# The first group of a fused mLSTM cell and feed-forward block: other landings, smaller turns and another order of loads

## The chip, the cores and the metric

The kernel runs on one core of a Trainium2 chip. The core has a matrix engine (TensorE, PE in the profile, with its weight loads as PEld), a vector engine (VectorE, DVE), an activation engine (ScalarE, ACT), a general engine (GpSimd, POOL) and a sync engine that mostly issues transfers (SyncE, SP). ScalarE issues transfers too; both queues are served by the core's 16 DMA engines. The metric is the device time of one execution in microseconds (us), lower is better.

## The reference

There are two blocks. The first is an mLSTM cell over B = 4 sequences, H = 8 heads, S = 768 steps, head size D = 40. The second is a feed-forward block (SwiGLU) on the 3072 tokens of width 320 that come out.

```python
for t in range(S):
    m_new = np.maximum(f_gate[:, :, t] + m, i_gate[:, :, t])
    f_stab = np.exp(f_gate[:, :, t] + m - m_new)
    i_stab = np.exp(i_gate[:, :, t] - m_new)
    m = m_new
    C = f_stab[..., None, None] * C + i_stab[..., None, None] * np.einsum('bhd,bhe->bhde', vt, kt)
    n = f_stab[..., None] * n + i_stab[..., None] * kt
    h_tilde = np.einsum('bhde,bhe->bhd', C, qt)
    nq = np.einsum('bhd,bhd->bh', n, qt)[:, :, None]
    denom = np.maximum(np.abs(nq), 1.0)
    o = 1.0 / (1.0 + np.exp(-o_gate[:, :, t]))
    y[:, :, t] = o * h_tilde / denom
...
x = y.transpose(0, 2, 1, 3).reshape(3072, 320)
g = x @ w_gate                                  # 320 x 1536
out = (g / (1 + np.exp(-g)) * (x @ w_val)) @ w_out   # 1536 x 320
```

The three weight matrices arrive as 64-bit floating point numbers, everything else in 32 bits.

## The kernel before

**Groups.** The kernel takes the 768 steps in six groups of 128 steps. A group is 128 steps of all four sequences, 512 tokens. Within a group the recurrence is written as matrix products: scores of keys against queries, weighted by a triangular matrix of exponentials (the intra part), plus the state that came in from the groups before. Each group then goes through the feed-forward block: twelve hidden steps m (128 of the 1536 hidden columns each), then the output projection.

**The order is written by hand.** A manual schedule is in force: every engine works through its instructions in the order in which the program names them, and each instruction waits on semaphores for what it needs. So a waiting instruction holds back all behind it on its engine, and the same is true for the transfers that an engine issues. Program order is therefore what sets the order of the work around the change.

**The first group** has no incoming state and is done by functions of its own (lines 520 to 665), which work on 16 (batch, head) pairs at a time, P = 0 and P = 1. Its parts:
- Transfers of k, q, v and o, 40 floats (160 bytes) per row, into tiles whose rows are padded: `k_sb` and `q_sb` have 64 columns per head, 40 used, `v_sb` has 41 with a one at the end.
- `first_mask`, `first_inputs`, `first_maxima` (531 to 541) put the exponents of the triangular weights in eight banks of PSUM, and `first_exp` (547) writes their exponentials to `W0`, which lies in the columns 0 to 7 of the tile `h_sb`.
- `first_turn` (561) transposes k and q on TensorE, two heads side by side, 128 rows at a time. Line 142 (ScalarE) or 144 (VectorE) copies the result out.
- `first_scores` (571) multiplies keys by queries, and line 575 multiplies the result into `W0`. `first_own` (582) multiplies `W0` by v, for one sequence u: 8 matmuls of 128 by 128.
- `first_x` (587 to 590) divides by the denominators, `sig` (515) takes the sigmoid of o, `first_gate` (596) multiplies by it and copies 64 columns behind the row as padding (597).
- `first_values` (552, 553) weights v by the last row, `first_state` (604) multiplies by k for the state that the next group gets, `first_kept` copies it out.
- `first_seam` (616) transposes x to `xT`, what the feed-forward block takes in.
- `burn` (521) are matmuls of no use to the result that keep TensorE at work; there are 7 at the start, and 3, 2 and 1 between the parts.

**The weights** are loaded in pieces (`piece_load`, 163 to 190): pieces 0 and 1 hold one hidden step each, 2 to 6 hold two each, 7 to 9 the output weights. The gate half of a piece goes to partitions 0 to 63, its val half, in two transfers, to partitions 64 to 127. SyncE issues the gate halves; ScalarE issues the val halves of pieces 0 to 4, SyncE those of 5 and 6. A piece lands as pairs of 32-bit words in one of two `raw` buffers, or, for pieces 2, 3 and 4, in parts of `h_sb` and `wo_sb` that are not yet in use. Then `convert` makes 32-bit floats of it: `scale` (ScalarE, 212 and 214), `join` (VectorE, 221 and 222), `rounded` (229, VectorE or GpSimd).

**The hidden steps** of the first group are the ten matmuls of line 706 for each m (20 rows of the profile, each over 512 tokens), the silu in 711, and the product in 712. `ahead[m]` names conversions and `slots[m]` all other work that goes between the steps: the loads for the second group, the late sums, maxima and decays of the state's scalars, and from slot 7 the weights of the second group. These are in `w_sb`: maxima go out to memory as `M_dram` (963), come back broadcast as two transfers (484), are subtracted (488), masked (493), taken to exponentials (512), multiplied by scores (360), and used by the `add` matmuls (379) between m = 10 and m = 11.

After the hidden steps comes `project_all` (723), and then the groups 1 to 5, which keep TensorE packed.

Of the kernel before, what the change touches and what calls it, by code (L numbers as in the profile page):

```python
# [24 lines left out]
def kernel(  # L25
# [135 lines left out]
    def piece_load(p, home=None):  # L161
        kind, m, n = PIECES[p]
        if kind == "gv":
            a, d = NKC, n * 128
            gate_w, val_w = (w[:, m * 128:(m + n) * 128].rearrange("(c p) f -> p c f", p=HP) for w in (moe_w_gate, moe_w_val))
            src = [(slice(0, HP), slice(0, NKC), gate_w), (slice(HP, 128), slice(0, NKC - 1), val_w[:, 1:]),
                   (slice(HP, 128), slice(NKC - 1, NKC), val_w[:, 0:1])]
            queues = (nc.sync,) + 2 * (nc.scalar if p < 5 else nc.sync,)
        else:
            a, d = n, DM  # L170
            src = [(slice(0, 128), slice(0, n), moe_w_out[m * 128:(m + n) * 128].rearrange("(a p) d -> p a d", p=128))]
            queues = (nc.sync,)
        if src[0][2].dtype == F32:
            for r, cs, w in src:
                if kind == "o":
                    nc.sync.dma_start(out=wo_sb[r, m:m + n, :], in_=w)
                else:
                    for x in range(n):
                        nc.sync.dma_start(out=wgv_sb[r, m + x, cs], in_=w[:, :, ts(x, 128)])
            return  # L180
        if home is None:
            raw = conv.tile([128, 4 * NKC * 128], U32, name="raw")
        else:
            raw = home.rearrange("p a t -> p (a t)").bitcast(U32)
        raw = raw[:, 0:2 * a * d]
        for (r, cs, w), queue in zip(src, queues):
            queue.dma_start(out=raw[r].rearrange("p (a d) -> p a d", a=a)[:, cs], in_=w.bitcast(U32))
# [47 lines left out]

    for P in range(2):
        load(k_sb, k, 0, P)
        load(q_sb, q, 0, P)
        load(v_sb, v, 0, P)
    load(o_sb, o_gate, 0, 0)  # L240
# [54 lines left out]
    def late_sums():  # L295
        nc.vector.tensor_tensor_scan(flat(f_sb), flat(keep1), flat(f_sb), 0.0, op0=ALU.mult, op1=ALU.add)
        nc.gpsimd.memset(step1, 0.0)
# [252 lines left out]

    def first_values(P):
        nc.gpsimd.tensor_copy(w_end[:, heads(P)], W0[:, heads(P), end])
        nc.gpsimd.tensor_tensor(vw_sb[:, heads(P)], v_sb[:, heads(P)], w_end[:, heads(P)].to_broadcast([128, UH, D1]),
                                op=ALU.mult)

    def first_turn(P, src, dst, engs):
        for b in range(2):
            tp = bank("tp_kq").rearrange("p (a t) -> p a t", t=L)
            for a in range(UA // 2):
                h = P * UH + b * H + 2 * a  # L560
                nc.tensor.transpose(tp[:, a, :], src[:, h:h + 2, :].rearrange("p h d -> p (h d)"), ident)  # L561
            a = P * UA + b * UA // 2
            copy(engs[b], dst[:, a:a + UA // 2, :], tp)
# [15 lines left out]
    def first_own(u):  # L579
        first_y[u] = bank("first_y", "gen")[:, 0:H * D1].rearrange("p (h d) -> p h d", d=D1)  # L580
        for h in range(H):
            nc.tensor.matmul(first_y[u][:, h, :], lhsT=W0[:, u * H + h, :], rhs=v_sb[:, u * H + h, :], start=True, stop=True)  # L582
# [10 lines left out]
    def first_gate(P):  # L593
        for u in (2 * P, 2 * P + 1):
            x = x_sb[:, u, 0:DM].rearrange("p (h d) -> p h d", d=D)
            nc.vector.tensor_tensor(x, x, o_sb[:, u * H:(u + 1) * H], op=ALU.mult)
        nc.gpsimd.tensor_copy(x_sb[:, 2 * P:2 * P + 2, DM:], x_sb[:, 2 * P:2 * P + 2, 0:HP])
# [12 lines left out]
    def first_seam(P, engs):  # L610
        for c, eng in zip(range(0, NKC, 2), engs):
            cs = range(c, min(c + 2, NKC))
            tp = bank("tp_x")[:, 0:len(cs) * 2 * L].rearrange("p (c u s) -> p c u s", u=2, s=L)
            for w in cs:
                for b in range(2):
                    nc.tensor.transpose(tp[:, w - c, b, :], x_sb[:, 2 * P + b, ds(w * HP, 2 * HP)], ident)
            copy(eng, xT(0)[:, c:c + len(cs), 2 * P * L:(2 * P + 2) * L].rearrange("p c (u s) -> p c u s", u=2), tp)

    burn(7)
    banks = [(u, j) for j in range(2) for u in range(B)]  # L620
    for f in (first_mask, first_inputs, first_maxima):
        for u, j in banks:
            f(u, j)
    first_exp(0)
    first_turn(0, k_sb, kT, (V, V))
    first_turn(0, q_sb, qT, (A, V))
    first_exp(1)
    first_values(0)
    first_scores(0)
    first_own(0)  # L630
    late_sums()
    first_turn(1, k_sb, kT, (A, A))
    first_x(0)
    first_turn(1, q_sb, qT, (A, V))
    load(o_sb, o_gate, 0, 1)
    piece_load(0)
    first_own(1)
    first_values(1)
    first_scores(1)
    first_x(1)  # L640
    sig(0)
    piece_load(1)
    burn(3)
    first_own(2)
    piece_load(2, h_sb[:, 1:1 + NKC])
    sig(1)
    burn(2)
    first_own(3)
    first_gate(0)
    first_x(2)  # L650
    first_x(3)
    first_gate(1)
    first_seam(0, (A, A, V))
    scale(0)
    ps1 = first_state(1, "gen")
    burn(1, "gen")
    piece_load(3, h_sb[:, NH - NKC:])
    join(0)
    first_seam(1, (A, A, V))
    rounded(0, V)  # L660
    first_kept(0, first_state(0), A)
    first_kept(1, ps1, V)
    convert(1, V)
    nc.scalar.activation(warm, warm, AF.Silu)
    piece_load(4, wo_sb)
    piece_load(5)
# [292 lines left out]
    def load_all(dst, a, n):  # L959
        for P in range(2):  # L960
# [10 lines left out]
        0: [run(convert, 2, V), run(late_maxima), run(load_all, k_sb, k, 1),  # L971
            run(nc.sync.dma_start, out=M_dram, in_=flat(M_sb)), run(load_all, q_sb, q, 1)],
        1: [run(piece_load, 6), run(late_decay)],
# [134 lines left out]
```

## Time and profile before

| | us |
|---|---|
| median of three runs | 512.71 (512.23 to 512.75) |
| the profiled execution, as timed | 513.3 |
| its span | 511.5 |
| TensorE busy | 505.1 (99%) |
| start of the first hidden step (line 706) | 31.92 |
| start of m = 11 of the first group | 88.04 |

The profiled execution ran at a granted clock of 0.999. The table's last two rows come from the trace. Busy times are sums over the whole span, and the first 32 us, the head, are a small part of it; for what goes on there, the chain of waits in a window and the table by stretches are read. A row of the chain is start, duration, engine, tile and line. A row of the timeline adds the shapes, and in brackets the idle time ahead of it with what ended it. A row of the table by stretches has the stretch, its length, busy time and instructions of TensorE, its weight loads, VectorE, ScalarE and GpSimd, the granted clock, the share of the DMA engines and GB/s.

### The profile page before, as it was taken

What the parts mean: (1) busy time and instruction counts of PE and PEld (TensorE: products, weight loads), DVE (VectorE), ACT (ScalarE), POOL (GpSimd) and SP (SyncE); (2) the same over time, 40 slices, a digit from 0 to 9 for tenths busy, and PEclk for the clock granted to TensorE, in tenths of its full rate; (3) what the DMA queues carried; (4) which work ended last, traced back from release to release, by engine and by line L of the source; (5) the groups of instructions that cost most, each with busy time, mean ns of one, the idle gap of its engine ahead of it and who ended that gap; (6) DMA issues with size and microseconds to landing.
All of it is one profiled execution on the core that took longest, in us unless ns stands there. A gap on an engine that the chain in (4) does not pass through costs nothing.

```text
span 511.5 us, 14788 instructions
## 1 busy us (share of the span) xinstructions
PE 505.1 (99%) x6307; PEld 428.8 (84%) x6309; DVE 332.3 (65%) x539; ACT 204.8 (40%) x394; POOL 255.0 (50%) x274
## 2 busy tenths in 40 slices
PE   8999999999999999999999999999999999999997
PEld 4964445667888899988899888899988899988896
DVE  5779767887897777687466678467658554233421
ACT  3477655448512339312339321338421340223210
POOL 1303427475879663367652457652447650166710
PEclk9999999999999999999999999999999999999999
DMA  9999999698502992501993411993101200000001
GB/s 123 174 232 238 168 194 244 148 177 119 88 1 45 143 130 39 92 3 26 156 134 42 75 21 27 156 131 43 42 3 19 37 3 27 27 1 0 1 14 38
DMA packets 205497, 43.27 MB, mean 85 GB/s; under 512 B 193432, under 2 KB 200600, under 8 KB 205432
## 3 DMA queue, kind: packets, MB, share of 16 engines
q1 hardware_dynamic: 203444, 39.49, 49.4%
q10 hardware_dynamic: 1988, 2.85, 2.4%
q8 instruction: 49, 0.80, 0.7%
q14 instruction: 16, 0.13, 0.1%
HBM read 35.68 MB, written 4.01 MB: 78 GB/s over the span
## 4 chain that ended last, share of the span: by engine, by line
PE 91%; DMA 2%; DVE 2%; issue 1%; POOL 1%; ACT 1%; SPq 0%; DVEq 0%; ACTq 0%; POOLq 0%
PE gv_x L854 26%; PE o_ps L777 23%; PE gv_y L854 21%; PE gv_ps L706 5%; PE o_ps L723 5%; DMA w_sb<-M_dram 2%; PE inter L402 2%; PE intra L411 2%; PE sp L353 2%; PE first_y L582 1%; PE add L379 1%; POOL w_sb L493 1%; PE burn L521 1%; PE tp_kq L561 1%; PE sp L571 1%
## 5 line engine op out<-in xcount | busy, mean ns | idle before, releaser
L854 PE MATMUL gv_x<-xT,wgv_sb 64*128 64x256 f32 x720 | 89.1, 377 | 0.0
L854 PEld LDWEIGHTS gv_x<-xT,wgv_sb 64*128 64x128 f32 x720 | 69.6, 187 | 7.9 <-issue 0.2
L777 PE MATMUL o_ps<-wo_sb,h_sb 128*128 128x160 f32 x480 | 67.4, 300 | 0.0
L777 PEld LDWEIGHTS o_ps<-wo_sb,h_sb 128*128 128x128 f32 x480 | 65.6, 190 | 1.7 <-issue 1.7
L902 ACT ACTIVATE h_sb<-gv_x 128x256 f32<-128x256 f32 x30 | 11.5, 383 | 117.8 <-PE gv_x L854 117.8
L706 PE MATMUL gv_ps<-xT,wgv_sb 64*128 64x512 f32 x240 | 53.7, 596 | 0.3 <-DVE wgv_sb L229 0.3
L706 PEld LDWEIGHTS gv_ps<-xT,wgv_sb 64*128 64x128 f32 x240 | 23.6, 187 | 24.4 <-issue 23.2
L854 PE MATMUL gv_y<-q_sb,wgv_sb 64*128 64x256 f32 x360 | 44.0, 377 | 0.0
L854 PE MATMUL gv_y<-xT,wgv_sb 64*128 64x256 f32 x360 | 43.9, 376 | 0.0
L854 PEld LDWEIGHTS gv_y<-q_sb,wgv_sb 64*128 64x128 f32 x360 | 34.9, 187 | 4.2 <-DVE tmp L894 0.4
L854 PEld LDWEIGHTS gv_y<-xT,wgv_sb 64*128 64x128 f32 x360 | 35.0, 187 | 3.9
L364 POOL TENSOR_TENSOR vw_sb<-v_sb,w_sb 128x656 f32<-128x656 f32 x10 | 14.6, 1467 | 41.2 <-ACT w_sb L509 40.0
L777 PE MATMUL o_ps<-wT,S 128*128 128x160 f32 x240 | 33.4, 299 | 0.0
L777 PEld LDWEIGHTS o_ps<-wT,S 128*128 128x128 f32 x240 | 32.9, 190 | 0.0
L509 ACT ACTIVATE w_sb<-w_sb,g_T 128x64 f32<-128x64 f32 x128 | 31.0, 334 | 0.0
L854 PE MATMUL gv_x<-q_sb,sw 64*128 64x256 f32 x240 | 31.0, 376 | 0.0
L875 POOL TENSOR_TENSOR h_sb<-x_sb 128x512 f32<-128x512 f32 x12 | 15.8, 1314 | 24.6 <-ACT x_sb L874 24.6
L895 POOL TENSOR_TENSOR tmp<-tmp 128x512 f32<-128x512 f32 x15 | 20.0, 1332 | 14.5 <-DVE tmp L894 14.5
L875 POOL TENSOR_TENSOR h_sb<-tmp 128x512 f32<-128x512 f32 x13 | 16.5, 1269 | 21.5 <-ACT tmp L874 21.5
L744 POOL TENSOR_TENSOR S<-h_sb 128x256 f32<-128x256 f32 x30 | 22.6, 752 | 9.2 <-DVE h_sb L875 7.3
L854 PE MATMUL gv_y<-q_sb,sw 64*128 64x256 f32 x200 | 27.0, 388 | 0.0
L723 PE MATMUL o_ps<-wo_sb,h_sb 128*128 128x320 f32 x96 | 26.9, 437 | 0.0
(221 smaller groups left out, 984.6 us busy)
## 6 DMA issues: line engine op xcount, KB each, us to landing
w_sb<-M_dram SPq DMA_DIRECT2D x10, 512.0 KB, 7.1
k_sb<-in_k_dram SPq DMA_DIRECT2D x12, 320.0 KB, 7.4
v_sb<-in_v_dram SPq DMA_DIRECT2D x12, 320.0 KB, 5.5
o_sb<-in_o_gate_dram SPq DMA_DIRECT2D x12, 320.0 KB, 6.8
raw<-in_moe_w_out_dram SPq DMA_DIRECT2D x3, 1280.0 KB, 7.5
x_sq<-k_sb SPq DMA_DIRECT2D x64, 40.0 KB, 2.0
q_sb<-in_q_dram SPq DMA_DIRECT2D x32, 64.0 KB, 3.8
out_dram<-tmp SPq DMA_DIRECT2D x24, 80.0 KB, 1.7
```

Source lines behind the costliest of these rows:

```text
L353: nc.tensor.matmul(sp[two][half(i), a, :], lhsT=kT[feats(two), P * UA + a, half(i)], rhs=qT[feats(two), P * UA + a, half(i)], start=True, ...
L364: eng.tensor_tensor(vw_sb[:, heads(P)], v_sb[:, heads(P)], w_sb[:, heads(P), last].to_broadcast([128, UH, D1]), op=ALU.mult)
L402: nc.tensor.matmul(inter[two][half(i), a, :], lhsT=qT[feats(two), P * UA + a, half(i)], rhs=state(2 * n + i)[feats(two), P * UA + a, :], s ...
L509: nc.scalar.activation(w_sb[:, h], w_sb[:, h], AF.Exp, bias=g_T[:, n, h:h + 1], scale=-1.0)
L706: nc.tensor.matmul(ps[i], lhsT=wgv_sb[half(i), m, kc, :], rhs=x[half(i), kc, :], start=(kc == 0), stop=(kc == NKC - 1))
L723: nc.tensor.matmul(ps[u], lhsT=hid(g, m)[:, ts(u, L)], rhs=wo_sb[:, m, :], start=(m == 0), stop=(m == NFC - 1))
L744: eng.tensor_tensor(S1[:, k], lo[:, second_half], hi[:, second_half], op=ALU.add)
L777: nc.tensor.matmul(node[x][:, i], lhsT=lhs(k)[:, ts(i, L)], rhs=rhs(k), start=start and k == 0 and i == 0, stop=stop and k == KH - 1, skip ...
L854: nc.tensor.matmul(ps[:, i, cols], lhsT=lhs(c)[half(i)], rhs=rhs(c)[half(i)], start=start and c == 0, stop=stop and c == n - 1, skip_group ...
L875: (nc.vector if k == KH - 1 else nc.gpsimd).tensor_tensor(h_sb[:, 2 * k + 1], uw[:, 0], uw[:, 1], op=ALU.mult)
L895: nc.gpsimd.tensor_tensor(uw[:, :, second_half], uw[:, :, second_half], uw[:, :, first_half], op=ALU.add)
L902: nc.scalar.activation(h[:, first_half], x[:, 0, first_half], AF.Silu)
```

## The change

All of it is in the first group and the order of loads around it.
- q and k of the first group land without padding (`load_dense`), in the columns 8 to 12 of `h_sb`; `spread` then copies them to the padded tiles: q of P = 0 on VectorE, the other three on GpSimd. The order of loads is q, k, q, k, v, v; before it was k, q, v, k, q, v. o of P = 0 and 1 follow behind the gate half of piece 0.
- `first_turn` is replaced by `turn_one`, and `first_seam` by `seam`, which the other groups use. They transpose blocks of 64 rows: 16 transposes per operand instead of 8, 20 per seam instead of 10.
- `first_own` makes each product in two column halves: 16 matmuls of 128 by 64 instead of 8 of 128 by 128.
- The burns between the parts go; the 7 at the start stay.
- The gates of P = 0 move from VectorE to GpSimd; the padding copy of P = 1 moves from GpSimd to ScalarE; the rounding of step 0's weights moves from VectorE to GpSimd.
- Copying the end weights out is a step of its own (`first_ends`), and so is what GpSimd does of the late sums (`late_differences`).
- Piece 1 is issued by SyncE alone, val halves too. Piece 2's last transfer is issued apart from the rest, and its conversion stands before the first hidden step instead of in slot 0. Pieces 4 and 5 are issued in slot 0, the late maxima, the store to `M_dram` and the q loads of the second group in slot 1.

```diff
-            queues = (nc.sync,) + 2 * (nc.scalar if p < 5 else nc.sync,)
+            queues = (nc.sync,) + 2 * (nc.scalar if p < 5 and p != 1 else nc.sync,)
...
+    dense = h_sb[:, NH - NKC:].rearrange("p m t -> p (m t)").rearrange("p (x h d) -> p x h d", x=4, d=D)
+    def load_dense(x, a, P):
+        nc.sync.dma_start(out=dense[:, x], in_=tokens(a, 0, P))
+    def spread(eng, x, dst, P):
+        copy(eng, dst[:, heads(P), 0:D], dense[:, x])
...
     for P in range(2):
-        load(k_sb, k, 0, P)
-        load(q_sb, q, 0, P)
+        load_dense(2 * P, q, P)
+        load_dense(2 * P + 1, k, P)
+    for P in range(2):
         load(v_sb, v, 0, P)
-    load(o_sb, o_gate, 0, 0)
...
     def first_own(u):
         for h in range(H):
-            nc.tensor.matmul(first_y[u][:, h, :], lhsT=W0[:, u * H + h, :], rhs=v_sb[:, u * H + h, :], start=True, stop=True)
+            for i in range(2):
+                nc.tensor.matmul(first_y[u][half(i), h, :], lhsT=W0[:, u * H + h, half(i)], rhs=v_sb[:, u * H + h, :],
+                                 start=True, stop=True)
...
+    spread(V, 0, q_sb, 0)
+    spread(G, 1, k_sb, 0)
     first_exp(0)
-    first_turn(0, k_sb, kT, (V, V))
-    first_turn(0, q_sb, qT, (A, V))
+    turn_one(0, q_sb, qT, (V, A))
+    turn_one(0, k_sb, kT, (V, A))
     first_exp(1)
+    first_ends(0)
+    spread(G, 2, q_sb, 1)
+    spread(G, 3, k_sb, 1)
+    first_scores(0)
+    turn_one(1, q_sb, qT, (A, A))
+    turn_one(1, k_sb, kT, (A, A))
     first_values(0)
-    first_scores(0)
+    late_sums()
+    piece_load(0)
+    load(o_sb, o_gate, 0, 0)
+    load(o_sb, o_gate, 0, 1)
     first_own(0)
-    late_sums()
-    first_turn(1, k_sb, kT, (A, A))
+    first_ends(1)
+    first_values(1)
+    late_differences()
+    first_own(1)
     first_x(0)
-    first_turn(1, q_sb, qT, (A, V))
-    load(o_sb, o_gate, 0, 1)
-    piece_load(0)
-    first_own(1)
-    first_values(1)
+    first_x(1)
     first_scores(1)
-    first_x(1)
     sig(0)
+    first_gate(0, (G, G), G)
+    scale(0)
+    first_own(2)
+    first_x(2)
+    sig(1)
+    ps0 = first_state(0)
+    first_own(3)
     piece_load(1)
-    burn(3)
-    first_own(2)
-    piece_load(2, h_sb[:, 1:1 + NKC])
-    sig(1)
-    burn(2)
-    first_own(3)
-    first_gate(0)
-    first_x(2)
+    seam(0, 0, (A, A, A, A))
     first_x(3)
-    first_gate(1)
-    first_seam(0, (A, A, V))
-    scale(0)
+    first_gate(1, (V, V), A)
+    join(0)
+    piece_load(2, h_sb[:, 1:1 + NKC], (0, 1))
+    rounded(0)
     ps1 = first_state(1, "gen")
-    burn(1, "gen")
+    seam(0, 1, (A, V, A, A))
+    piece_load(2, parts=(2,))
+    scale(1)
+    first_kept(0, ps0, V)
+    join(1)
+    first_kept(1, ps1, A)
+    rounded(1, V)
     piece_load(3, h_sb[:, NH - NKC:])
-    join(0)
-    first_seam(1, (A, A, V))
-    rounded(0, V)
-    first_kept(0, first_state(0), A)
-    first_kept(1, ps1, V)
-    convert(1, V)
     nc.scalar.activation(warm, warm, AF.Silu)
-    piece_load(4, wo_sb)
-    piece_load(5)
+    convert(2, V)
...
-        0: [run(convert, 2, V), run(late_maxima), run(load_all, k_sb, k, 1),
-            run(nc.sync.dma_start, out=M_dram, in_=flat(M_sb)), run(load_all, q_sb, q, 1)],
-        1: [run(piece_load, 6), run(late_decay)],
+        0: [run(piece_load, 4, wo_sb), run(piece_load, 5), run(load_all, k_sb, k, 1)],
+        1: [run(late_maxima), run(nc.sync.dma_start, out=M_dram, in_=flat(M_sb)), run(load_all, q_sb, q, 1),
+            run(piece_load, 6), run(late_decay)],
```

More of the change, by code (lines that the diff above doesn't have):

```diff
@@ L159, with piece_load @@
     PIECES = [("gv", 0, 1), ("gv", 1, 1)] + [("gv", m, 2) for m in range(2, NFC, 2)] + [("o", m, 4) for m in range(0, NFC, 4)]
-    def piece_load(p, home=None):
+    homes = {}
+    def piece_load(p, home=None, parts=(0, 1, 2)):
         kind, m, n = PIECES[p]
@@ L173, in piece_load @@
         if src[0][2].dtype == F32:
-            for r, cs, w in src:
+            for r, cs, w in [src[x] for x in parts if x < len(src)]:
                 if kind == "o":
@@ L180, in piece_load @@
             return
-        if home is None:
+        if p in homes:
+            raw = homes[p]
+        elif home is None:
             raw = conv.tile([128, 4 * NKC * 128], U32, name="raw")
@@ L184, in piece_load @@
             raw = home.rearrange("p a t -> p (a t)").bitcast(U32)
-        raw = raw[:, 0:2 * a * d]
-        for (r, cs, w), queue in zip(src, queues):
+        raw = homes[p] = raw[:, 0:2 * a * d]
+        for (r, cs, w), queue in [(src[x], queues[x]) for x in parts if x < len(src)]:
             queue.dma_start(out=raw[r].rearrange("p (a d) -> p a d", a=a)[:, cs], in_=w.bitcast(U32))
@@ L296, in late_sums, with late_differences @@
         nc.vector.tensor_tensor_scan(flat(f_sb), flat(keep1), flat(f_sb), 0.0, op0=ALU.mult, op1=ALU.add)
+    def late_differences():
         nc.gpsimd.memset(step1, 0.0)
@@ L549, with first_ends @@
     w_end = early.tile([128, BH, 1], F32)
+    def first_ends(P):
+        nc.gpsimd.tensor_copy(w_end[:, heads(P)], W0[:, heads(P), end])
     def first_values(P):
-        nc.gpsimd.tensor_copy(w_end[:, heads(P)], W0[:, heads(P), end])
         nc.gpsimd.tensor_tensor(vw_sb[:, heads(P)], v_sb[:, heads(P)], w_end[:, heads(P)].to_broadcast([128, UH, D1]),
                                 op=ALU.mult)
[L556 to L563, printed above, removed]
     def first_scores(P):
@@ L591, in first_x, with first_gate @@
                                 den.to_broadcast([128, H, D]), op=ALU.mult)
-    def first_gate(P):
-        for u in (2 * P, 2 * P + 1):
+    def first_gate(P, engs, pad):
+        for u, eng in zip((2 * P, 2 * P + 1), engs):
             x = x_sb[:, u, 0:DM].rearrange("p (h d) -> p h d", d=D)
-            nc.vector.tensor_tensor(x, x, o_sb[:, u * H:(u + 1) * H], op=ALU.mult)
-        nc.gpsimd.tensor_copy(x_sb[:, 2 * P:2 * P + 2, DM:], x_sb[:, 2 * P:2 * P + 2, 0:HP])
+            eng.tensor_tensor(x, x, o_sb[:, u * H:(u + 1) * H], op=ALU.mult)
+        copy(pad, x_sb[:, 2 * P:2 * P + 2, DM:], x_sb[:, 2 * P:2 * P + 2, 0:HP])
     def first_state(P, tag="cell"):
@@ L608, in first_kept @@
         copy(eng, state(2)[:, P * UA:(P + 1) * UA], ps)
[L610 to L617, printed above, removed]
     burn(7)
```

## The prediction, before the run

> **What bounds the kernel now.** I read the page's busy shares first, then the chain of waits in the head, then the timeline around the one place where the tensor engine still waits later, and last the table by stretches for the transfers. All times are from the profiled execution: span 511.5 us, 513.3 us as timed, so 1.8 us lie outside the span. The median of the three runs is 512.71, and I subtract what I find from that.
>
> ```profile
> PE 505.1 (99%) x6307; PEld 428.8 (84%) x6309; DVE 332.3 (65%) x539; ACT 204.8 (40%) x394; POOL 255.0 (50%) x274
> ```
>
> TensorE is busy 99% of the span. From the first feed-forward matmul (gv_ps, line 706) at 31.92 on, its program is nearly packed, and the change leaves that program alone. So only two things can move the time: the start of that matmul, call it S, and the waits behind it. The chain of waits shows what sets S:
>
> ```profile
> 23.14 1.71 PE first_y L582 x16
> 24.85 0.43 PE burn L521 x2
> 25.28 1.73 PE first_y L582 x16
> 27.00 0.02 issue
> ...
> 27.67 0.49 DVE x_sb L590
> 28.16 0.80 DVE x_sb L596 x2
> 28.96 0.33 DVE xT L144
> 29.29 0.51 DVE wgv_sb L221
> 29.80 0.02 issue
> 29.82 0.82 DVE wgv_sb L222
> 30.65 0.06 DVE xT L144
> 30.71 0.26 issue
> 30.96 0.82 DVE wgv_sb L229
> 31.79 0.14 issue
> 31.92 2.38 PE gv_ps L706 x9
> ```
>
> TensorE carries the chain until the last first_own ends at 27.00. Then VectorE does everything in a row for 4.9 us: denominators, x, two gates, the first weight piece's join and rounding.
>
> From 31.92 the twelve hidden steps follow each other every 4.29 us, with the group's other matmuls between. The one real hole is between m = 10 and m = 11, in the timeline:
>
> ```profile
> 72.75 2.36 DVE L488 TENSOR_TENSOR w_sb<-g_T,w_sb 128x1024 f32<-128x1024 f32 x2 [0.89 <-DMA w_sb<-M_dram]
> 74.05 6.76 POOL L493 TENSOR_SCALAR_AFFINE_SELECT w_sb<-w_sb 64x1024 f32<-64x1024 f32 x4 [11.97 <-DVE w_sb L488]
> ...
> 83.84 0.69 DVE L712 TENSOR_TENSOR h_sb<-tmp,gv_ps 128x512 f32<-128x512 f32 x1 [3.44 <-ACT tmp L711]
> ...
> 84.44 2.47 DVE L360 TENSOR_TENSOR w_sb<-sp,w_sb 128x512 f32<-128x512 f32 x4
> ```
>
> The second load of w_sb lands at 72.66 (call it T); the subtraction had idled 0.89 us for it. Subtract, mask, exponential, a table load, silu, product and weighing then run without slack. The add matmuls (line 379, 1.41 us when packed) are stretched over 85.27 to 88.04, where m = 11 starts, 15.38 us after T. If T had been early enough, the subtraction would have followed the product of m = 7 by 0.89 us less, so m = 11 cannot come before S + 55.3 (87.2 here, from 88.04 less the 0.89 of idle). Hence
>
> m = 11 starts at the later of S + (any stall of an earlier step) + 55.3 and T + 15.38.
>
> In before the second binds, and everything after m = 11 moves with it. A head that is faster without an earlier T gains nothing.
>
> **The change, part by part: the head.** *Loads.* Landings of before: k0 8.5, q0 11.0, v0 12.8, k1 15.2; q1 and v1 have gaps in their records and I put them by the packets at 17.5 and 19.6. The new order is q0, k0, q1, k1, v0, v1 on the same SP queue with the same 160-byte source rows, and in stretches of 150 GB/s whether destination rows are padded (k) or nearly dense (o took no less than k). So I give the dense landing nothing (k took 2.4 us of transfer and o 1.7, so it may give up to 0.7 us a load), and take the same six slots: 8.5, 11.0, 12.8, 15.2, 17.5, 19.6. The spread copies (four of 128x640) cost 0.49 us on VectorE (its row for such a size, L590); for POOL I take 0.75, by L805's 0.87 for a two-operand pass and 0.29 for 128x128, with 1.3 (L553's) as the upper end. All are hidden in waiting for loads.
>
> *TensorE.* Per operand, sixteen 64-row transposes for eight 128-row ones: L318's rows take 0.45 us start to start against 0.92 to 1.09, four times, 2.1 us less. first_own: the row of the same shape as its new one, 128*64, is first_state:
>
> ```profile
> L582 PE MATMUL first_y<-v_sb,h_sb 128*128 128x41 f32 x64 | 7.8, 279 | 0.2 <-DVE h_sb L575 0.2
> ...
> L604 PE MATMUL add<-vw_sb,k_sb 128*64 128x41 f32 x64 | 2.3, 231 | 0.0
> ```
>
> Thirty-two of the latter took 1.13, sixteen of the former 1.76: 0.6 less, four times. Six burns at 0.215 go, 1.3. Together 5.9 us of work off a path of 16.6 (10.38 to 27.00): TensorE stops being the head's bound, and the loads take its place. First_own(0), at 15.13 in before, now waits for v0 at 17.5; by the rows above the order then gives own1 at 18.7, scores of the second half 19.8 to 21.9, VectorE's two products (1.3 per bank), own2 22.4, state 23.6, own3 24.6 to 25.9.
>
> *VectorE and POOL behind it.* x3 1.1 us (L587 to L590), to 27.0; two gates of 0.48, to 27.9; join 0.51 + 0.82, to 29.3. Rounding moves to POOL: 1.55 us there for VectorE's 0.82, so +0.7, to 30.85. Beside it run the seam copies, now mostly on ACT: 64-row seam 0.77 against 1.27, its copies 0.59 each, done by 30.5. The first gate of the second half is behind the sigmoid of o1; o0 and o1 are now queued behind q, k, v and piece 0, and land near 23.6 and 25.5 (before 21.25 and 24.57). Sigmoid 0.74 makes 26.6, 0.4 us ahead of its use. If o1 came 1 us later, S would be 0.6 later. ACT's first two val halves are issued in its program after v0 and v1, where in before they went at 18.3: hidden, as piece 0 is first needed at 27.9 on VectorE. POOL's two gates (0.87 each, x0 done by 20.4) lie behind the differences (0.62 + 1.53) and end near 26: seam 0 needs them, TensorE is at own3 then, so cover is there but thin.
>
> S becomes 30.85 (before 31.92): 1.1 less. Bounds: 30.7, where VectorE's own sequence sets it, and 32.5, with o1 2 us late.
>
> **Behind the head.** *Piece 2.* Its val halves go out on ACT after the gates, near 28.9 and 30.5 (before 24.67 and 26.27); its conversion is before hidden(0,0) in the engines' programs. In before they needed 7 to 9 us behind a full queue; with piece 1's val on SP the ACT queue is empty, so I put the landing near 36. Step m = 2 starts 3.8 us after (scaling 1.6, join 1.36, rounding 0.82): 39.8, against 39.45 when packed. Stall 0.3; bounds 0 and 2.
>
> *T.* Transfers run without a pause from 3 to 72 us, so T moves with the rate at which the same bytes go ahead of it. The table by stretches:
>
> ```profile
> 27.00:36.00 9.00, 8.56 (x104) 6.32 (x105) 7.17 (x15) 7.33 (x12) 0.29 (x1) 1.00 1.07 216
> 36.00:42.00 6.00, 6.00 (x32) 3.10 (x30) 4.68 (x8) 4.06 (x6) 0.00 (x0) 1.00 1.05 326
> 42.00:48.00 6.00, 6.00 (x32) 2.74 (x30) 5.86 (x12) 4.38 (x6) 2.44 (x2) 1.00 1.07 213
> ```
>
> The last column is GB/s. In 36 to 42 SP's gate halves (partitions 0 to 63) and ACT's val halves (64 to 127) of pieces 3 and 4 were in flight together: 326. From 42 on SP is alone on one half: 213. Now val 2 also comes late enough to go beside gate 2: the piece's 0.66 MB at 326 is 2.0 us, at 216 3.0, so at least 1 us is saved; piece 1, all on SP, goes at 200 to 216 either way. Everything behind piece 5 (k, M_dram, q, piece 6, w_sb) is SP's alone as before. T = 71.5, with 69 as the lower end if pieces 2 to 4 all overlap in full. The k loads pass late_maxima, M's store and q in the order, but the store is still issued behind k on SP in both, so I count nothing for that.
>
> The Trainium skill speaks against this. Its page "SBUF — State Buffer", section "Can I just issue two DMAs to hit both halves?", says that two concurrent transfers, one on each half of the partitions, gain only 6%. The row of 326 against 213 in this trace disagrees. By the row T is 71.5 and m = 11 starts at 86.9; by the page's 6%, as an estimate, the 1.96 MB of that stretch take 8.7 us instead of 6 wherever it isn't repeated, T is 75.3 and m = 11 starts at 90.7. Its mechanism is the third rival.
>
> **Sum.** S + 0.3 + 55.3 = 86.45; T + 15.38 = 86.9. The later, 86.9, less 88.04 is 1.15 us; a little more if T is under 71. I take 1.3: 512.71 - 1.3 = 511.4. The most is 1.6 to 2 (S 30.7, no stall, T below 71): 510.7.
>
> **The rivals.**
> *No earlier T.* The bytes are the same and the queues were full. Then m = 11 stays at 88.0, the hole between m = 10 and 11 grows by what the head gained: 512.7. For it: only 0.66 MB changes its neighbour.
> *Piece 2 late (slower).* If its val lands behind other queued packets, m = 2 waits. The gain is gone once it lands after 37.5 (stall 1.9); at 38.6 the loss is 1 us; behind gate 3 at 40.6, as gates landed in before, m = 2 starts at 44.4 and S + 4.9 + 55.3 = 91.05, a loss of 3: 515.7. For it: val transfers took 7 to 11 us from issue in before. Likely value near 38.8: 513.9.
> *The halves take turns (slower).* If all of pieces 2 to 4 ran at 213, as 27 to 36 did with both queues in use, the 1.96 MB of 36 to 42 take 9.2 us for 6: T = 75.8, m = 11 at 91.2, 515.9. Decides from T above 72.7. Against it: the row of 326.
> *The clock falls without burns.* Clock reads 1.00 throughout, over gaps of at most 0.3 us; now TensorE waits over a us for v0, and more before the seams. If it fell, by the first stretch (full speed 4.4 us after the first burn) I price half rate over 4.4 us, 2.2 us: S = 33.0, m = 11 at 88.6: 513.3. The Trainium skill's page "TensorE: Matmul & The Clock Gate", Part 1, section "HAM oscillation — how this bites in real kernels", puts the idle time from which the clock drops at some 3.4 us; no gap that I expect is so long.
> *It doesn't do what it says.* The head stays bound by 160-byte rows and late o: S = 31.9, m = 11 at 87.5: 512.2.
>
> **How the numbers follow.** Forecast 0.48; no earlier T 0.19; piece 2 late 0.15; halves take turns 0.07; clock 0.05; no faster head 0.06. A change within 0.2%, about 1 us, can't be told from none here. Faster: the forecast with most of its spread, 0.48. Same: no earlier T, no faster head, the clock, 0.28. Slower: the rest, 0.24. The range leaves out the halves' case and the worst of piece 2: 510.4 to 514.6; the forecast's own is 510.6 to 512.1.
>
> **What would show it.** First gv_ps at 30.85 and first_own(0) at v0's landing, near 17.5; no burns in the head and the clock at 1.00; m = 2 at 39.8; over 300 GB/s from about 30 to 42; w_sb's subtraction no later than 72; m = 11 at 86.9. I am wrong if gv_ps starts later than 32, if any hidden step before m = 8 waits over 1 us for its weights, or if w_sb lands at 72.7 or later.

## The result, and the profile after

The changed kernel takes 519.02 us (median of 6 runs, 517.77 to 520.2) against 513.11 for the kernel before (6 runs, 512.23 to 516.74). The ratio is 1.0107, with an interval of 1.0079 to 1.0136: slower by 5.9 us. The profiled execution took 520.03 us, its span is 518.2.

The page's first lines, then its row of the granted clock over 40 equal slices of the span:

```profile
span 518.2 us, 15018 instructions
PE 505.3 (98%) x6419; PEld 427.2 (82%) x6419; DVE 329.4 (64%) x534; ACT 205.9 (40%) x400; POOL 260.2 (50%) x279
...
PEclk9988999999899999999999999999999999999999
```

TensorE is busy for 505.3 us, where it was 505.1, in a span longer by 6.7 us. And the clock is below full in three slices, 26 to 52 us and 130 to 143 us, where in the kernel before it was full throughout.

TensorE's own timeline from the last seam to the end of the fourth hidden step (line 714 is what was line 706):

```profile
26.74 0.34 PE L490 MATMUL tp_x<-ident,x_sb 64*128 64x64 f32 x3 [0.68 <-ACT xT L142]
27.01 1.13 PE L613 MATMUL add<-vw_sb,k_sb 128*64 128x41 f32 x32
28.07 0.77 PE L490 MATMUL tp_x<-ident,x_sb 64*128 64x64 f32 x17
29.60 0.34 PE L490 MATMUL tp_x<-ident,x_sb 64*128 64x64 f32 x3 [0.76 <-DVE xT L144]
30.26 10.32 PE L714 MATMUL gv_ps<-xT,wgv_sb 64*128 64x512 f32 x40 [0.32 <-POOL wgv_sb L233]
42.75 11.05 PE L714 MATMUL gv_ps<-xT,wgv_sb 64*128 64x512 f32 x40 [2.18 <-DVE wgv_sb L233]
```

The first hidden step starts at 30.26, earlier than the 31.92 of before by 1.66. But two hidden steps take 10.3 us where they took 8.7, then TensorE waits 2.18 us for the weights of m = 2, and the next two take 11.0 where they took 8.7. The chain of waits in this stretch begins with the landing of those weights:

```profile
30.03 9.33 DMA h_sb<-in_moe_w_val_dram
39.36 0.02 issue
39.38 0.04 ACTq L216
39.42 0.04 issue
39.47 0.79 ACT top L216
...
41.78 0.84 DVE wgv_sb L233
42.61 0.14 issue
42.75 2.38 PE gv_ps L714 x5
```

The val half of piece 2 was issued at 27.30 and 30.03 and landed at 39.36; before it was 24.67 and 26.27, and 35.44. SyncE's next gate halves went the other way: those of pieces 3 and 4 were issued at 24.59 and 26.82, before at 28.91 and 29.55. The table by stretches (stretch, its length, busy time of the five engines, clock, DMA share, GB/s) shows the clock:

```profile
26.40:29.80 3.40, 2.30 (x55) 2.05 (x55) 3.04 (x7) 1.89 (x6) 1.13 (x1) 1.00 1.07 213
29.80:33.20 3.40, 3.08 (x11) 1.40 (x10) 1.66 (x4) 2.92 (x6) 0.40 (x1) 0.50 1.08 203
33.20:40.00 6.80, 6.80 (x34) 2.96 (x32) 0.63 (x1) 1.31 (x3) 0.00 (x0) 1.00 1.04 293
40.00:43.40 3.40, 1.22 (x7) 0.44 (x5) 2.94 (x5) 3.08 (x6) 0.00 (x0) 1.00 1.06 222
43.40:46.80 3.40, 3.40 (x11) 2.15 (x11) 3.26 (x6) 1.64 (x3) 1.54 (x1) 0.51 1.20 175
```

Each time in this table that TensorE (the first busy figure) was busy for only 1.2 to 2.3 of some 3.4 us, the next 3.4 us ran at half clock. By these rows that costs about 1.7 us if TensorE is busy all through.

The third place is in group 1, in the chain of waits there:

```profile
129.88 3.77 DMA out_dram<-x_sb
133.65 0.09 DVE kT L357
...
134.81 1.20 DVE kT L357
136.01 0.37 DVE C L409
...
138.46 0.51 DVE C L409
138.97 0.14 issue
139.10 3.64 PE gv_x L862 x16
```

TensorE waits 2.25 us for VectorE's eight additions to the state (line 409), these are behind VectorE's transposes of k (line 357), and these waited until 133.64 for the last of 16 small loads of k (`raw<-in_k_dram`, landed at 133.42; the chain names a store issued right behind it). The half clock follows again, from 139 to 142.5.

Put together, by TensorE's starts in the two traces:

| until | before | after | difference |
|---|---|---|---|
| first hidden step | 31.92 | 30.26 | -1.66 |
| end of m = 3 | 49.31 | 53.73 | +4.42 |
| m = 11 | 88.04 | 91.69 | +3.65 |
| group 1's add | 125.75 | 128.69 | +2.94 |
| group 1, behind the wait at 137 | 135.64 | 142.56 | +6.92 |
| end of the last projection | 507.83 | 514.54 | +6.71 |

The head gains 1.66. The first four hidden steps lose 6.08. Two waits of before that were hidden in this delay give back 0.76 (w_sb) and some 0.7 (intra and inter). Group 1 loses 2.25 by waiting and 1.7 by the clock.

### The profile page after: what moved, and what is told of

The parts are those of the page before. It is cut to its first block, busy times and chain, and to the rows that moved or that the text cites. A ratio compares the mean times of both kernels' runs of the same rounds, so it can differ in the third digit from the quotient of the medians.

```text
span 518.2 us, 15018 instructions
## 1 busy us (share of the span) xinstructions
PE 505.3 (98%) x6419; PEld 427.2 (82%) x6419; DVE 329.4 (64%) x534; ACT 205.9 (40%) x400; POOL 260.2 (50%) x279
## 4 chain that ended last, share of the span: by engine, by line
PE 86%; DMA 3%; SPq 2%; DVE 1%; issue 0%; POOL 0%; ACT 0%; DVEq 0%; ACTq 0%
PE gv_x L862 25%; PE o_ps L785 22%; PE gv_y L862 20%; PE gv_ps L714 9%; PE o_ps L731 3%; PE inter L416 2%; PE sp L367 2%; SPq L351 2%; PE intra L425 2%; DMA h_sb<-in_moe_w_val_dram 2%; PE add L393 1%; DMA out_dram<-x_sb 1%; DVE C L409 1%; POOL wo_sb L233 0%; PE tp_kq L332 0%
## 5 line engine op out<-in xcount | busy, mean ns | idle before, releaser
L862 PE MATMUL gv_x<-xT,wgv_sb 64*128 64x256 f32 x720 | 90.6, 381 | 2.2 <-DVE C L409 2.2
L714 PE MATMUL gv_ps<-xT,wgv_sb 64*128 64x512 f32 x240 | 57.5, 625 | 2.5 <-DVE wgv_sb L233 2.2
L714 PEld LDWEIGHTS gv_ps<-xT,wgv_sb 64*128 64x128 f32 x240 | 25.9, 197 | 28.1 <-issue 22.4
L862 PEld LDWEIGHTS gv_y<-xT,wgv_sb 64*128 64x128 f32 x360 | 35.1, 187 | 3.9
```

The lines of the kernel that those rows point to most:

```text
L714: nc.tensor.matmul(ps[i], lhsT=wgv_sb[half(i), m, kc, :], rhs=x[half(i), kc, :], start=(kc == 0), stop=(kc == NKC - 1))
L862: nc.tensor.matmul(ps[:, i, cols], lhsT=lhs(c)[half(i)], rhs=rhs(c)[half(i)], start=start and c == 0, stop=stop and c == n - 1, skip_group ...
```

## The experiments

A ratio is against runs of the kernel before on the same chip, with its interval. "S" is the start of the first hidden step, "gate 2" and "val 2" are the gate half and the val half of piece 2, and groups are counted from 0, so that group 1 is the second.

**Piece 2 ahead of the others (e1).** The val halves of piece 2 go out on SP, right behind gate 2.

```diff
-            queues = (nc.sync,) + 2 * (nc.scalar if p < 5 and p != 1 else nc.sync,)
+            queues = (nc.sync,) + 2 * (nc.scalar if p < 5 and p not in (1, 2) else nc.sync,)
...
-    piece_load(2, h_sb[:, 1:1 + NKC], (0, 1))
+    piece_load(2, h_sb[:, 1:1 + NKC])
...
-    piece_load(2, parts=(2,))
```

> The change with the val halves of piece 2 issued by SP right behind gate 2, ahead of gates 3 to 5; nothing else. Theory (piece 2 was late behind what SP had issued ahead of it): its val lands by about 35.5 instead of 39.4, the 2.2 us wait ahead of m = 2 goes, and with it the second half-clock window (1.7 us); the first one, at 29.4 to 32.9, stays. m = 2 starts near S + 8.6 + 1.7 = 40.6 instead of 42.75, and m = 11 at 88 to 88.4, set by w_sb (72.97 + 15.38 in the changed kernel). Time 515 if the hole in group 1 at 137 stays, 513 if it goes. Rival (the wait is of little weight, the hole in group 1 with its half-clock window is the loss by itself): 517 to 518.

Measured: 514.54 us, ratio 0.9997 (0.9967 to 1.0027); span of the profiled run 510.2. Piece 2 landed at 35.18, S is 30.65, the first four steps take 17.37 us, and m = 11 starts at 86.56, 1.5 us earlier than in the kernel before (88 was expected, with `w_sb` landing at 72.97; it landed at 71.18). In this trace the first half-clock window did not come either, which the expectation had left in. The trace is that of the fastest of e1's ten runs, though: six of the others have a granted clock of 0.992 or 0.993, about what two half-clock windows of 3.4 us make of such a span. By the median of the ten, this one edit takes away the loss. The group 1 wait is down to 0.28 us in this trace; that the edit would do this was not expected, and the runs below take it up.

```profile
core 0: us, PE busy (x) PEld busy (x) DVE busy (x) ACT busy (x) POOL busy (x), PEclk, DMA share, GB/s
27.00:34.00 7.00, 5.78 (x71) 3.70 (x73) 5.13 (x9) 5.41 (x13) 1.53 (x1) 1.00 1.06 224
34.00:41.00 7.00, 7.00 (x34) 3.24 (x32) 4.70 (x9) 4.04 (x6) 0.58 (x1) 1.00 1.05 256
41.00:48.00 7.00, 7.00 (x34) 2.90 (x30) 6.80 (x13) 5.36 (x8) 2.51 (x2) 1.00 1.06 249
```

This is e1's table by stretches: full clock, and TensorE busy for the whole of 34 to 48.

**The fault put into the kernel before (e6).** There the val halves of piece 2 are held back until piece 3 has been issued.

```diff
...
+            if p == 2 and x:
+                held_back.append(issue)
...
     piece_load(3, h_sb[:, NH - NKC:])
+    for issue in held_back:
+        issue()
```

> The kernel before with one fault put in: the val halves of piece 2 are issued behind piece 3, near 29.5, all else as it was. Theory (the order of issue of this one piece is the loss): val 2 lands near 40, m = 2 starts at 43 to 44 instead of 40.6, TensorE stands for 2 to 3.5 us, the clock halves for one window of 3.4 us (1.7 us); the hole at w_sb takes back about 0.9, so 4 to 5 us more by group 1, 516.5 to 518.5 on the count of 513. Rival (it was the other parts of the change): within 1.5 us of the kernel before.

Measured: 523.42 us, ratio 1.0166 (1.0126 to 1.0206). The direction is as expected, the size is not: SP was now free to issue gates 3 and 4 at 25.2 and 25.9 (28.9 and 29.6 before), so the val half landed at 43.7 to 44.8, TensorE waited 6.56 us ahead of m = 2, and two half-clock windows followed. Val 2 also stood behind val 3 on ScalarE's own queue, so this fault is larger than that of the changed kernel. Alone in the kernel before, it costs more than the whole change did.

**Why it is late: order or engine.** Four kernels. In e2, gates 3 and 4 are issued by ScalarE behind val 2. In e5 all of pieces 3 to 5 are, and val 2's two halves go together. In e13 the k loads for group 1 are also moved from slot 0 to slot 1, behind the store of the maxima. In e14 val 2 is on SP, but behind gate 3.

```diff
# e2
+            queues = (nc.scalar if p in (3, 4) else nc.sync,) + 2 * (nc.scalar if p < 5 and p != 1 else nc.sync,)
# e5
+            queues = (nc.scalar if p in (3, 4, 5) else nc.sync,) + 2 * (nc.scalar if p < 6 and p != 1 else nc.sync,)
# e13: e5, and
-        0: [run(piece_load, 4, wo_sb), run(piece_load, 5), run(load_all, k_sb, k, 1)],
+        0: [run(piece_load, 4, wo_sb), run(piece_load, 5)],
...
# e14: queues as in e1, and
...
+    piece_load(3, h_sb[:, NH - NKC:], (0,))
+    piece_load(2, parts=(1, 2))
+    piece_load(3, parts=(1, 2))
```

> The change with gates 3 and 4 issued by ScalarE, so behind the val halves of piece 2, which keep their late place at 27.3 and 30.0. If val 2 was late because SP had run ahead with gates 3 and 4, it lands by about 35.5 and m = 2 starts near 40.6, as with the val halves on SP. Rival (val 2 was late because of its own late issue, some 9 to 11 us ahead of landing): it lands at 38.5 and 39.4 as before and m = 2 stays at 42.7, 518 to 519.

> The change with pieces 3, 4 and 5 issued by ScalarE whole, so behind piece 2's val halves, which keep ScalarE's late place (27.3 and now right behind). Nothing but gate 2 and piece 1 is issued ahead of val 2. Theory (transfers of both queues are served in the order of issue; val 2 landed at 39.4 because gates 3, 4 and 5, 1.97 MB, went ahead): val 2 lands at 34 to 35.5, m = 2 waits for under 0.5 us. Rival (its own late issue or ScalarE's queue delays it by 9 to 11 us): it lands at 37 to 39, and m = 2 waits for 1.5 us or more.

> As the kernel with pieces 3 to 5 on ScalarE behind val 2, and with the k loads of group 2's first half and second half too moved back, from slot 0 to slot 1 behind the store of the maxima, so that SP has nothing at all to issue between gate 2 and val 2 (there a k load of 320 KB went ahead and another was mixed in, and val 2 landed at 37.7 and 38.6). Order of issue: val 2, issued at its late place near 27.7 and 28.4 on ScalarE, starts when gate 2 is through, near 31.7, and lands at 34.5 to 35.5. Lateness of ScalarE itself: it lands at 37 to 39 again.

(Its "group 2" is the second group, group 1 in the count used here.)

> The change with the val halves of piece 2 on SP, so issued early (near 25.5 to 27), but behind gate 3. Order of issue: gate 2, gate 3 and val 2 follow each other at 200 GB/s, 3.3 us each, so val 2 lands at 38 to 39, though it was issued 1 to 3 us earlier than in the changed kernel; m = 2 waits until 42. Lateness of ScalarE: with an early issue on SP it lands near 35 to 36 as when it was ahead of gate 3, and there is no wait at m = 2.

Measured, with the issues and landings of val 2's halves:

| kernel | issued | issued ahead of it, behind gate 2 | landed |
|---|---|---|---|
| changed kernel | 27.30, 30.03 | gates 3 and 4; gate 5 ahead of the second half | 38.54, 39.36 |
| e2 | 27.70, 30.55 | gate and val of piece 5 | 40.27, 40.98 |
| e5 | 27.77, 28.48 | one k load | 37.72, 38.59 |
| e13 | 27.43, 28.08 | nothing | 34.49, 35.10 |
| e14 | 26.40, 28.09 | gate 3 | 38.03, 38.68 |
| e1 | 25.23, 25.98 | nothing | 33.97, 35.18 |

e2's time was 521.57, ratio 1.0137 (1.01 to 1.0174): it emptied SP of gates 3 and 4, and SP went on with piece 5 at once. The run meant to show the order spoilt itself, as e5 did with k loads (529.49 us in one run; a later wait of 10.2 us, ahead of m = 3, with all pieces issued by ScalarE, is most of that and was not followed up). e13 and e14 tell the two causes apart. In e13 the first, larger half goes out from ScalarE as late as in the changed kernel (27.43, 27.30) and lands 4 us earlier. In e14 both halves go out earlier and from SP, behind gate 3, and are as late as ever. (e13 took 518.89 us and e14 515.22 in their one run; in both the head had two half-clock windows, in e14 they hid the expected wait at m = 2, and e13 had a group 1 wait of 2.66 us.) So what counts is what has been issued ahead, on either queue, and not the engine that issues. The DMA view of the changed kernel, from val 2's issue until it starts to move and from there to its landing (packets, MB, share of 16 engines), in two answers:

```profile
q1 hardware_dynamic: 675, 1.32, 104.9%
```

```profile
q1 hardware_dynamic: 440, 0.86, 56.0%
q10 hardware_dynamic: 413, 0.78, 48.6%
```

From 27.3 to 34 only q1, SP's queue, moves: 1.32 MB, the end of piece 1 (landed at 28.47), gate 2 (31.79) and most of gate 3 (35.09). q10, ScalarE's, has val 2 waiting and gets nothing. From 34 to 39.4 both move side by side. The order of issue is not kept strictly: gate 4, issued 0.5 us ahead of val 2, goes beside it and lands at 38.82.

**The clock (e3, e4).** Burns in the seam's waits: 3, 3 and 2.

```diff
...
+    def fill(n):
+        for _ in range(n):
+            nc.tensor.matmul(hot_bank, lhsT=junk[:, 0:128], rhs=junk, start=True, stop=True)
...
-    seam(0, 0, (A, A, A, A))
+    seam(0, 0, (A, A, A, A), lambda: fill(3))
...
-    seam(0, 1, (A, V, A, A))
+    seam(0, 1, (A, V, A, A), lambda: fill(3))
+    fill(2)
```

> The change with 8 burn matmuls (0.215 us each) put into TensorE's waits between and behind the seam's transposes, 3, 3 and 2. Theory (the clock fell at 29.4 because in the 3.4 us before it TensorE stood for 1.3 us and transposed for 1.1): the clock stays 1.00 up to the wait ahead of m = 2, S near 30.3. As m = 2 is set by piece 2's landing at 39.4 and starts at 42.7 either way, the wait grows from 2.2 to about 3.9 us and the time stays within 0.5 us of the changed kernel, 518.5 to 519.5. Rival (the half-clock window at 29.4 costs its 1.7 us at the end): 517.3.

> Both: val 2 on SP behind gate 2, and the burns. Theory: S near 30.3, clock 1.00 throughout, m = 2 at S + 8.6 = 38.9, 1.7 us before that of the kernel with val 2 on SP alone; whether this is worth anything at the end depends on w_sb's landing: at 72.97 m = 11 can't come before 88.35, so the time equals that of val 2 on SP alone within 0.5 us. Rival (w_sb's landing moves with the head): m = 11 near 86.9 and 1 to 1.5 us less than with val 2 on SP alone.

Measured for e3: 518.35 us, ratio 1.0074 (1.0047 to 1.0102). The table by stretches of e3:

```profile
26.40:29.80 3.40, 3.24 (x60) 2.33 (x59) 3.17 (x7) 1.90 (x6) 1.04 (x1) 1.00 1.07 220
29.80:33.20 3.40, 3.40 (x19) 1.53 (x18) 1.67 (x4) 2.95 (x6) 0.50 (x1) 1.00 1.07 202
33.20:40.00 6.80, 6.02 (x30) 2.37 (x26) 0.60 (x1) 1.28 (x3) 0.00 (x0) 1.00 1.05 289
40.00:43.40 3.40, 0.66 (x3) 0.45 (x5) 2.95 (x5) 3.08 (x6) 0.00 (x0) 1.00 1.06 201
43.40:46.80 3.40, 3.40 (x11) 2.30 (x11) 3.26 (x6) 0.98 (x3) 1.53 (x1) 0.54 1.21 177
```

The first half-clock window is gone, and nothing is won: the wait ahead of m = 2 grows to 3.52 us, m = 2 starts at 42.74, as in the changed kernel, and the window behind that wait stays. As long as piece 2 is late, the clock in the head is free. e4: 513.84 us, ratio 1.0003 (0.9976 to 1.0031), S 31.00, the same as e1. The two traces can't say more than that, since e1's had no half-clock window to remove. The other runs can: the granted clock is 0.996 or more in all ten of e4, against 0.992 or 0.993 in six of e1's ten, and the time is the same. With o's loads where they are, the windows in the head cost nothing that these runs could show, with intervals of 1.5 us to either side.

**The wait in group 1 (e7, e8, e15, e9).** The loads of o for group 2, 0.65 MB, go behind the small loads of k; in the kernel before (e7), with e1's edit (e8), in the changed kernel (e15), and with e1's edit and the burns (e9).

```diff
-        3: [run(do_divide, 1, 1), run(load_all, o_sb, o_gate, 2), run(early_squares, 0), run(weights_cap, 0)],
+        3: [run(do_divide, 1, 1), run(early_squares, 0), run(load_all, o_sb, o_gate, 2), run(weights_cap, 0)],
```

> The kernel before with the loads of o for group 2 issued behind the 16 small loads of k (the squares) instead of ahead of them. Theory (the hole in group 1 near 131 and its half-clock window come when the last of these small loads lands late, and they wait behind 0.65 MB of o): the loads start near 112 instead of 116.9, VectorE's transposes start some 4 us earlier against TensorE, no hole and no half-clock window there, the spread of the runs shrinks to under 1 us, and the median falls to 512 to 512.5 from 513 to 514.6. Rival (the hole has another cause): median and spread unchanged.

> The change with piece 2's val halves on SP and with the loads of o for group 2 behind the small loads of k. Theory: what the head gained, 1.3 us at the end of the span, now stays: 511 in nearly all runs, 1.0 to 1.5 us below the kernel before with the same move of o. Rival (the head's gain is lost at another wait): equal to the kernel before with that move, within 0.5 us.

> The changed kernel with nothing but the loads of o for group 2 put behind the small loads of k, so that the wait in group 1 near 137 goes; the wait at m = 2 stays. If the loss of 5.9 us was made of the wait at m = 2 with its half-clock windows (some 3.5 us at the end of the first group, net of the head's gain) and of the wait in group 1 with its window (2.2 + 1.7): 515 to 516. If the wait in group 1 is an accident of the one profiled run: within 1 us of the changed kernel's 519.

> All three repairs of the change: val 2 on SP, burns in the seam's waits, o for group 2 behind the small loads. In the run without the burns the clock was halved for two windows behind the seam (6.8 us at half speed, some 3.4 us lost) and the span was still 510.3. Theory: no half-clock window in the head, S near 30.5, m = 2 at 39, and 1 to 2 us less than without the burns: 510.5 to 511.5, 0.5 to 0.8% below the kernel before. Rival (the head is hidden behind w_sb's landing whatever it gains): equal to the run without the burns, 512 to 512.4.

| kernel | median, us | ratio (interval) |
|---|---|---|
| e7, before with o later | 514.20 | 0.9998 (0.9972 to 1.0024) |
| e15, changed kernel with o later | 514.72 | 1.0015 (0.9994 to 1.0035) |
| e8, val 2 on SP, o later | 512.40 | 0.9954 (0.9928 to 0.9980) |
| e9, val 2 on SP, burns, o later | 511.39 | 0.9933 (0.9905 to 0.9961) |

The wait in group 1 is gone from all four traces. For the changed kernel this is worth most of its loss: from 1.0107 to 1.0015, 0.92% or 4.7 us, though its wait at m = 2 (2.31 us) stands. So that wait was no accident of one profiled run. For the kernel before it is worth nothing, against what I expected: its spread stays (512.34 to 517.99), and its trace has a wait of 1.40 us in front of line 402 instead, at 95.15 us, for which the profile names no cause. e9's trace has one of 2.44 us at the same place (line 416 there, at 93.24), with a half-clock window behind it; it is that of the slowest of e9's runs, 514.51, the others being 510.27 to 511.87. So this is another place that is just in time, and it was not followed up. e8 is 1.8 us below e7, where 1.0 to 1.5 was expected, so the head's gain is there once this place is cleared. e9 beats the kernel before by 0.67% (3.4 us), where the changed kernel is 1.07% above it; e9 lies 1 us below e8, which is what was expected of the burns now that piece 2 is early, but the two intervals overlap, so that share is not shown.

VectorE's transposes start by the last landing, and TensorE's wait follows from that start. Counted from the first add of group 1:

| kernel | transposes start | TensorE waits, us |
|---|---|---|
| before | 2.2 | 0 |
| e1 | 3.0 | 0.28 |
| e12 | 3.5 | 0.75 |
| e2 | 3.7 | 1.04 |
| e3, e11 | 4.2 | 1.53 |
| changed kernel | 5.0 | 2.25 |
| e13 | 5.4 | 2.66 |
| e15 | 0.4 | 0 |

The wait is the start less 2.7 us in each. The kernel before stands 0.5 us short of it. What makes the last of the small loads land at 2.0 us in one execution and at 5.1 in another, I did not find: their issue differs by 0.9 us at most (-0.1 to 0.8), the rest is in the landing of the last of them, and e13, with no wait at m = 2, has the longest.

**What the head is made of (e10, e11, e12).** Three parts undone, on top of e1 (S 30.65).

```diff
# e10: no dense landing, no spread
-        nc.sync.dma_start(out=dense[:, x], in_=tokens(a, 0, P))
+        load((q_sb, k_sb)[x % 2], a, 0, P)
# e11: first_own in 8 matmuls of 128 by 128
# e12: first_turn and first_seam of the kernel before in place of turn_one and seam
```

> The change with val 2 on SP (S 30.65), and with q and k loaded straight into their padded tiles, no spread copies. Theory (the dense landing is what brought k of the second half to 12.9 from 15.2): q and k land at 8.5, 11.0, 12.8, 15.2, v0 near 17.5, v1 near 19.6, and S is 0.3 to 1 us later, near 31.2. Rival (the rate was higher for another reason, the order): landings within 0.3 us of the dense ones, S 30.5.

> The change with val 2 on SP, and first_own as before in 8 matmuls of 128 by 128. TensorE is the bound of the head from 10.4 to 25: 0.6 us more for each of four, S 2 to 2.5 us later, 32.7 to 33.1. Rival (the loads are the bound of the head): S within 0.7 us of 30.65.

> The change with val 2 on SP, and the turns and seams as before with 128 rows at a time. With TensorE as the bound: 0.5 us more for each of four turns and of two seams, S 2 to 3 us later, 32.7 to 33.6. Rival (the turns wait for loads and the seams for VectorE): S within 0.7 us of 30.65.

Measured, in one run each: S is 32.98, 37.09 and 31.76. All three expectations missed. In e10 and e12, as in e1, the chain of waits into S runs through the val half of piece 0: ScalarE's program scales it ahead of the sigmoid of o's second half, and the scaling waits for its landing. Sigmoid, gates, join and rounding follow.

| kernel | val half of piece 0 landed | rounding ended | S |
|---|---|---|---|
| e1 | 24.45 | 30.60 | 30.65 |
| e12 | 25.65 | 31.71 | 31.76 |
| e10 | 26.09 | 32.15 | 32.98 |

e10: the landings of q and k moved as foretold (8.94, 10.96, 13.37, 15.67; dense in e1 8.02, 9.22, 11.01, 12.80), and with them what is queued behind, the val half by 1.6 us. The rest of the 2.3 us at S is the half clock, which came at 29 us and stretched TensorE's last work ahead of S (the 32 matmuls of line 613 took 1.93 us, in e1 1.13). e11: first_own 0 and 1 took 5.06 us in place of 2.00, as the clock was at half from 20 to 27 without any wait ahead of it:

```profile
15.80:19.20 3.40, 2.88 (x42) 2.45 (x42) 3.40 (x4) 2.10 (x4) 1.85 (x3) 1.00 1.22 178
19.20:22.60 3.40, 3.40 (x23) 3.40 (x23) 1.77 (x5) 2.07 (x3) 2.59 (x3) 0.66 1.03 172
22.60:26.00 3.40, 3.40 (x30) 3.32 (x31) 1.66 (x6) 1.84 (x3) 1.50 (x3) 0.50 1.16 208
```

TensorE is busy 2.9 and then 3.4 of 3.4 us, and the clock falls and stays down. e12: S is later by 1.1 us and the val half by 1.2, with the same loads ahead of it, and TensorE stood for 1.76 us ahead of S. So the wide turns and seams did not set S there. Part of the turns' time was spent waiting anyway (TensorE waits 0.82 us ahead of the first scores with narrow turns, 0.35 with wide ones). Why the val half landed later, I did not find.

## Why the prediction was wrong

I forecast 511.4, range 510.4 to 514.6; it is 519.0. (The chances of the rivals add up to 0.30 for "same" and 0.22 for "slower", where I wrote 0.28 and 0.24.)

- **The head: right in its sum, in part by luck.** S was forecast 30.85 and measured 30.26, and the bound named for it held: VectorE's denominators, x, gates and join follow each other from 25.33 on, and the rounding behind them. But two terms were wrong and cancelled. I gave the dense landing nothing (in one paragraph I had o taking no less than k, and k taking 2.4 us and o 1.7); k of the second half landed at 12.87, not 15.2. In return I had put o's second half at 25.5 for padded landings, where it came at 27.1 (e10); with dense ones it came at 25.35. Two more readings failed. TensorE did not stop being the bound: first_own(0) started at 17.8 behind its own queue, not at v0's landing. And the val half of piece 0 is not hidden, as I had it: in e1, e10 and e12 S hangs on its landing.
- **The step that failed: piece 2.** "With piece 1's val on SP the ACT queue is empty, so I put the landing near 36." An empty queue is no help while what the other queue issued earlier is still to be moved, and SP had issued gate 3 at 24.59, 2.7 us ahead of val 2. I counted nothing for that. The landing was 39.36, and the wait was 2.18 us, not 0.3. The second rival had the place and the mechanism (it named 38.8 as its likely value), with a chance of 0.15, and its price of 513.9 left out what follows such a wait: a half-clock window and later waits. e1, with this order repaired, loses nothing.
- **The clock: a rival with 0.05.** It needed no gap of 3.4 us, the figure of the Trainium skill's page "TensorE: Matmul & The Clock Gate", in "Part 1: The HAM clock gate". In the changed kernel waits of 0.33 and 0.76 us among transposes, in 3.4 us, came ahead of the fall in the head, and some 2.2 us of waiting twice behind it. The same page of the Trainium skill, in "Part 4: PE-mode transpose", says that transposes don't count as busy in the same way. That fits most heads here: 1.2 of TensorE's 2.3 busy us in the changed kernel were transposes, and burns kept the clock up: without them it fell in the head in nine of the ten profiled kernels with 64-row turns, and in e12 with wide ones, with them in none of three (e3, e4, e9). It is not the whole rule: e1's trace has the same transposes and 2.34 of 3.4 us busy (26.4 to 29.8) and kept its clock, and e11 lost it with hardly a wait. The price of 1.7 us per window was never set against a wait, though every wait of 2 us on TensorE brought one.
- **T and m = 11: the numbers came out in e1, but not for the reason given.** There the subtraction of `w_sb` starts at 71.27 (forecast T 71.5) and m = 11 at 86.56 (forecast 86.9), and the trace's last projection ends 1.3 us earlier than that of before, the 1.3 that I forecast. But val 2 did not go beside gate 2 there, from which I had worked out T: it followed on the same queue, and 27 to 36 us ran at 218 GB/s, before at 216. What ran faster was 3 to 15 us, with the dense landing, at 181 GB/s against 153; that is 0.34 MB more, by my estimate 1.6 us at 210 GB/s, and T gained 1.5. In e10, with padded landings, it was 150 and `w_sb` landed at 74.28. This is likely and not shown: e7, with the head of before, has T at 71.55. In the changed kernel itself T was 72.97, later than the 72.66 of before. It did not bind: its m = 11 is S + 55.3 + the 6.1 us lost in the first four steps, as in the formula.
- **The two halves of the partitions: the row was right.** Where both queues moved, it was 293 GB/s (33.2 to 40), against 203 for SP alone (29.8 to 33.2). The 6% that the Trainium skill's page "SBUF — State Buffer" gives for two halves, in "Can I just issue two DMAs to hit both halves?", is not what this case shows. But overlap was not to be had where I counted on it, since val 2 waited its turn behind gate 3.
- **Not seen at all: group 1.** I took everything behind m = 11 as packed, from a trace with a wait of almost nothing at that place. It had half a us of room. The runs put this at 4.7 of the 5.9 us (e15), and it is likely what blurs e1, which has a faster head in its trace and yet the time of before, since with o moved (e8) the gain shows.

The two parts don't add up as if they were apart: repairing piece 2 alone takes away 1.1%, moving o alone 0.9%, of a loss of 1.07%; both, 1.5%. Part of what either removes must then be lost or hidden elsewhere without the other; where, no trace here was followed to show.

## What to carry to other kernels

When loads move in a program, list the issue time of every transfer on every queue, in order, and add up the bytes ahead of the one that is needed next: an engine that runs free will issue its later pieces ahead of another queue's urgent one. For every wait on TensorE that the change may open, price the half clock behind it as well as the wait. And ask of each place that the trace shows as just in time how far it is from being late, since a gain in front of it, or a jitter of 1 us, may fall over that edge.

## What the runs showed of the hardware that was not expected

- Two queues, one order: from 27.3 to 34 us ScalarE's queue had 0.5 MB waiting and moved nothing, while SP's moved 1.32 MB at 200 GB/s that had been issued earlier. In e13, with the first half issued from ScalarE at the same time and nothing of SP's behind gate 2, it was through at 35.1. It is not strictly one order: gate 4, issued 0.5 us ahead of val 2, was moved beside it. The Trainium skill's page "DMA: Bandwidth & Descriptors", section "Queues, rings and completion order", has each engine take turns between the queues by packets; from 27.3 to 34 us the packets here did not, until gate 3 was nearly through.
- The granted clock falls in steps of about 3.4 us, to half (0.50 from 29.8 to 33.2, 0.51 from 43.4 to 46.8 in the changed kernel), and 2.2 us of TensorE's waiting was enough for it in each trace that has such a wait. Waits of 1.53 us in group 1 (e3, e11) brought no fall there. With hardly a wait (two of 0.26 us in 15.8 to 19.2) it fell in e11, in transposes and first_own matmuls of 128 by 41 columns. Why there and not in the kernel before, which has the same matmuls in another order, stays open.
- Rows of 160 bytes land faster when they lie without gaps in the destination: 168 and 178 GB/s (5 to 10 and 10 to 15 us, e1) against 140 and 141 (e10), all other loads being the same; the changed kernel has 176 and 173, the kernel before 140 and 146.
